# Bucketed attention and two gated layers on one core: P x V in bursts of two groups, the bucket projection in float32 column tiles, other ranks

## The chip, the cores and the metric

One core of a Trainium2 chip runs the whole program. The metric is the device time of one execution in microseconds. Three executions of the kernel before took 786.24, 788.03 and 2870.33 us; the median is 788.03 us. A fourth execution, the profiled one, took 786.92 us.

## The reference

Two batches of eight heads, 768 positions, head size 64. Each query and key gets a 6-bit bucket from the signs of its projection; only pairs of one bucket attend. Two dense layers follow over 1536 tokens, 512 wide inside and out, 2048 in the middle.

```python
q_bits = (einsum('bhsd,dk->bhsk', q, proj) > 0); k_bits likewise
mask   = q_bucket[:, :, :, None] == k_bucket[:, :, None, :]
scores = where(mask, scale * q @ k.T, -1e9)
attn   = softmax(scores); x = attn @ v                       # float32
h = x @ w_in;  P = a0 + a1 h + a2 h^2 + a3 h^3;  Q = 1 + |b0||h| + |b1|h^2
x = (P / (Q + 1e-6)) @ w_out
h = x @ w_in2; out = (h * clip(h + 3, 0, 6) / 6) @ w_out2
```

All inputs and the output are float32.

## The kernel before

**Attention** is cut into 48 groups, `group(g)`: head g // 3, 256 query rows, handled as two tiles of 128 rows (rr = 0, 1). Per group: S, four matmuls per row tile (`s_mm`, L326 and L329); M, the row maximum on DVE (L333); E, the exponential on ACT (L55, p<-s); NV and A, small sums; N, the normalisation of a 128x768 tile on POOL (L354), twice; P, twelve transposes on TensorE (`p_mm`, L362, tiles tt); H, three copies of the transposed tiles out of PSUM on ACT or DVE (`p_copy`, L55 and L372, tiles pt); V, twelve float32 matmuls (`v_mm`, L380), which put the two row tiles in two column halves of the array, 64 columns each; OC and VA, copies of the result on ACT and DVE; for odd heads XH and XL, the split into a high and a low part on POOL (L403, L409).

**Heads** come in pairs, `pair(pr)`. Per head: LQ, loads of q and k; TP, six transposes (`tp_mm`, L215); TH, the rounded high part by ACT (two halves of 384); TL, the low part by DVE (two halves, L58, tl<-tp,qsc,th). Per pair: Z, the projection onto the six directions, in the high and low parts: twelve 384-column matmuls over the whole array (`z_mm`, L254); ZB, the comparison to bits on DVE (L259, two halves). SPH, SPL and SB are DMAs on SP's queue that copy high parts, low parts and bits into the operands q1, q2, k1, k2 of the scores; all of them stand in SP's queue in one order.

**Layers.** There are 96 steps of 24 matmuls of 512 columns (L432 in, L500 out). Weights are converted from raw float32 to two rounded parts, in 64 units: two passes on ACT (L110, L114), a shift on DVE (L119), an addition on POOL (L123), the high part on ACT or POOL (L131, L133), the low part on DVE or POOL (L138). The first NPRE units have room during attention, the next NMID when its early buffers are released.

**What sets the order.** All work is put in a table with a rank (group number times `W_SLOT` plus an offset `OFF`), engines with costs `W`, and dependencies. `ordered()` places the lowest rank that is ready on a free engine of its model and writes each engine's instructions in that order. On the chip each engine goes through its own list in order and waits for what the next instruction needs. Buffers are rings: four PSUM banks "T" are shared by tp, z, tt and o; two double banks "S" hold scores; six pt tiles hold transposed probabilities. `start()` writes head 0 by hand; `fill` puts in a few matmuls on zeros.

Of the kernel before, what the change touches and what calls it, by code (L numbers as in the profile page):

```python
# [14 lines left out]
NB = 6  # L15
# [10 lines left out]
NPRE = 11  # L26
NMID = 8
WARM = 8
CVS = (1, 2, 5, 11, 17, 23, 29, 35, 39, 42, 43)
RING = {"raw": 3, "cvd": 3, "t1": 2, "t2": 3, "t3": 2, "t4": 1, "gh": 2, "gl": 2}  # L30

W = {"S": 0.70, "M": 0.87, "E": 0.89, "NV": 0.53, "A": 0.28, "N": 0.97, "P": 0.44, "H": 0.59, "H_D": 0.66, "V": 1.4, "OC": 0.30,
# [8 lines left out]
W_SLOT = 4.7626  # L41

OFF = {"S": -2.838, "rr": 3.521, "M": -6.776, "E": -11.597, "NV": -11.654, "A": -3.446, "N": -8.05, "P": 10.877, "H": -13.583, "V": 14.339,
       "OC": -19.289, "VA": -4.457, "XH": 12.347, "XL": -6.444, "TP": 13.65, "Z": 6.62, "c": 2.102, "SPH": -7.318, "SPL": -23.623, "SB": -8.428,
       "LQ": -20.758, "LV": 0.663, "ld": -12.347, "cf": 7.841}
AHEAD = 3.8243
FILL = {("TP", 1, 1): 3, ("S", 1, 1): 6}
RINGS = {"T": 4, "S": 2, "p": 6, "pt": 6}


def body(tc, q, k, v, proj, moe_w_in, moe_w_out, moe_a, moe_b, moe2_w_in, moe2_w_out, out):
    nc = tc.nc

    def act(out, in_, func=ACTF.Copy, **kw):
        nc.scalar.activation(out=out, in_=in_, func=func, **kw)  # L55
# [85 lines left out]
    nat, spl, hl, lr, live = {}, {}, {}, {}, {}  # L141
# [54 lines left out]
    for _ in range(WARM):  # L196
        nc.tensor.matmul(out=warm, lhsT=zfill[:, 0:128], rhs=zfill[:, 128:512], start=True, stop=True)

# [9 lines left out]
    thr = cpool.tile([128, 2], F32, name="thr")  # L208

# [8 lines left out]
    def tp_hi(hd, n):  # L218
        if n == 0:
            hl[hd] = tuple(ate.tile([128, S], F32R, name=f"t{x}", tag=f"t{x}{hd % 2}") for x in "hl")  # L220
        act(hl[hd][0][:, n * 384:(n + 1) * 384], live[("tp", hd, n)], scale=qsc)

    def tp_full(hd, n):
        full = live[("tf", hd, n)] = ate.tile([128, 384], F32, name="tf", tag="tf", bufs=2)
        act(full, live.pop(("tp", hd, n)), scale=qsc)

    def tp_lo(hd, n):
        th, tl = (t[:, n * 384:(n + 1) * 384] for t in hl[hd])
        if ("tf", hd, n) in live:
            nc.gpsimd.tensor_tensor(out=tl, in0=live.pop(("tf", hd, n)), in1=f(th), op=ALU.subtract)  # L230
        else:
            stt(tl, live.pop(("tp", hd, n)), qsc, f(th), ALU.mult, ALU.subtract)
# [14 lines left out]
    def z_mm(pr, n, heads=(0, 1)):  # L247
        z = live[("z", pr, n)] = psum.tile([128, 384], F32, name="z", tag="T", bufs=4)
        ops = []
# [6 lines left out]
    def z_bits(pr, n):  # L256
        if n == 0:
            live["bt"] = ate.tile([128, S], F32R, name="bt")
        nc.vector.tensor_scalar(out=live["bt"][:, n * 384:(n + 1) * 384], in0=live.pop(("z", pr, n)), scalar1=thr[:, 0:1],  # L259
                                scalar2=thr[:, 1:2], op0=ALU.is_gt, op1=ALU.mult)  # L260

    def spread_bits(hd):
        for i in range(2):
            o = 64 * (hd % 2) + 32 * i
            nc.sync.dma_start(out=f(lr[hd][2 * i + 1])[64:KP], in_=f(live["bt"])[o:o + 2 * NB])
# [7 lines left out]
    def start():  # L273
# [21 lines left out]
        for n in range(2):  # L295
            z_mm(0, n, (0,))
            z_bits(0, n)
# [537 lines left out]
```

## Time and profile before

| | us |
|---|---|
| median of three executions | 788.03 |
| profiled execution, device time | 786.92 |
| its span, first to last instruction | 785.1 |
| TensorE matmul busy | 771.5 (98%) |
| TensorE weight load busy | 654.2 (83%) |
| DVE busy | 553.9 (71%) |
| ACT busy | 482.0 (61%) |
| POOL busy | 352.5 (45%) |

The span falls into attention (to about 260 us), and the layers after it, which begin to mix in from 246 us. A busy share over the whole span mixes the two, so the rows further down are cut by stretch. Matmul ends are modelled; where a price is wanted, the difference between starts in the timeline is the safer reading.

### The profile page before, as it was taken

How to read it: one execution, taken by the hardware profiler on the slowest of the kernel's cores; microseconds unless marked ns; L12 is line 12 of the kernel's file. 1: busy time of each engine (PE TensorE's matmuls, PEld its weight loads, DVE VectorE, ACT ScalarE, POOL GpSimd, SP SyncE). 2: the span in 40 equal slices, each digit the busy share in tenths (PEclk: the TensorE clock that was granted, in tenths of full speed). 3: DMA queues.
4: the chain of work that ended last, by engine and by line, in shares of the span. 5: the costliest groups of instructions: out<-in, count | busy, mean ns of one | idle time of the engine just before them, and what ended most of it. 6: DMA issues, size and time to landing. Idle time of an engine off the chain costs nothing.

```text
span 785.1 us, 12730 instructions
## 1 busy us (share of the span) xinstructions
PE 771.5 (98%) x4629; PEld 654.2 (83%) x4629; DVE 553.9 (71%) x927; ACT 482.0 (61%) x893; POOL 352.5 (45%) x413
## 2 busy tenths in 40 slices
PE   8999999999999999999999999999999999999997
PEld 7888989999998887788888888888888888888886
DVE  7898988887788999999989999987622322232222
ACT  6887976677767888966557789887522322222221
POOL 3798985665677746722224476876500000000000
PEclk9999999999999999999999999999999999999999
DMA  7986786465330324400002033336100100010001
GB/s 190 228 223 166 195 217 152 116 144 121 75 86 21 114 82 131 125 14 1 0 1 78 4 108 108 108 108 198 69 1 1 54 1 1 1 53 1 1 0 55
DMA packets 46767, 65.78 MB, mean 84 GB/s; under 512 B 28808, under 2 KB 30856, under 8 KB 46704
## 3 DMA queue, kind: packets, MB, share of 16 engines
q1 hardware_dynamic: 45920, 64.76, 29.8%
q8 instruction: 37, 0.61, 0.3%
q10 hardware_dynamic: 784, 0.20, 0.1%
q14 instruction: 26, 0.21, 0.1%
HBM read 43.00 MB, written 3.15 MB: 59 GB/s over the span
## 4 chain that ended last, share of the span: by engine, by line
PE 85%; DVE 8%; ACT 4%; DMA 2%; issue 1%; POOL 1%; SPq 0%; ACTq 0%; POOLq 0%
PE h L432 30%; PE acc L500 30%; PE tt L362 8%; PE o L380 8%; PE s L326 4%; PE s L329 3%; DVE t L58 3%; PE z L254 2%; PE tp L215 1%; DVE stat L333 1%; DVE cvd L119 1%; ACT t L55 1%; DVE wo_0l L138 1%; DMA q<-th 1%; DVE r L58 1%
## 5 line engine op out<-in xcount | busy, mean ns | idle before, releaser
L354 POOL TENSOR_SCALAR p<-p,stat 128x768 f32<-128x768 f32 x96 | 95.7, 1004 | 35.4 <-DVE stat L350 21.7
L58 DVE SCALAR_TENSOR_TENSOR t<-t,h 128x512 f32<-128x512 f32 x48 | 33.1, 689 | 107.7 <-ACT t L55 107.7
L55 ACT ACTIVATE t<-h,cbias 128x512 f32<-128x512 f32 x48 | 33.1, 689 | 122.7 <-PE h L432 122.7
L123 POOL TENSOR_TENSOR cvd<-cvd,raw 128x512 int32<-128x512 int32 x64 | 89.2, 1396 | 42.1 <-DVE cvd L119 20.1
L489 POOL TENSOR_TENSOR gl<-t,gh 128x512 fp32r<-128x512 f32 x48 | 63.3, 1318 | 98.2 <-ACT gh L55 90.8
L55 ACT ACTIVATE p<-s,stat 128x768 f32<-128x768 f32 x96 | 85.9, 899 | 11.7 <-DVE stat L333 10.3
L333 DVE TENSOR_REDUCE stat<-s 128x1 f32<-128x768 f32 x96 | 89.4, 953 | 3.8 <-PE s L329 2.4
L55 ACT ACTIVATE gh<-t 128x512 fp32r<-128x512 f32 x96 | 60.5, 630 | 47.7 <-PE acc L500 41.6
L362 PE MATMUL tt<-ident,p 128*128 128x128 f32 x576 | 84.7, 277 | 1.4 <-DVE bt L259 0.9
L362 PEld LDWEIGHTS tt<-ident,p 128*128 128x128 f32 x576 | 66.7, 140 | 11.8 <-issue 5.1
L380 PE MATMUL o<-pt,nv 128*64 128x128 f32 x1152 | 73.5, 277 | 0.3 <-DVE bt L259 0.3
L489 DVE TENSOR_TENSOR gl<-t,gh 128x512 fp32r<-128x512 f32 x48 | 37.5, 781 | 51.3 <-PE acc L500 47.8
L58 DVE SCALAR_TENSOR_TENSOR t<-t,coef,h 128x512 f32<-128x512 f32 x96 | 71.4, 744 | 1.7
L380 PEld LDWEIGHTS o<-pt,nv 128*64 128x64 f32 x1152 | 61.9, 137 | 10.0 <-issue 6.1
L58 DVE SCALAR_TENSOR_TENSOR t<-t,r 128x512 f32<-128x512 f32 x96 | 65.8, 685 | 4.7 <-ACT r L55 2.3
L372 DVE COPY pt<-tt 128x512 f32<-128x512 f32 x75 | 50.7, 686 | 25.0 <-PE tt L362 24.7
L55 ACT ACTIVATE pt<-tt 128x512 f32<-128x512 f32 x69 | 40.8, 595 | 39.5 <-PE tt L362 39.0
L326 PE MATMUL s<-k,q 128*128 128x384 f32 x192 | 56.1, 373 | 1.7 <-ACT p L55 1.7
L500 PE MATMUL acc<-gh,wo_0h 128*128 128x512 f32 x192 | 54.6, 391 | 2.2 <-ACT gh L55 2.2
L500 PE MATMUL acc<-gl,wo_0h 128*128 128x512 f32 x192 | 54.4, 390 | 0.0
L500 PE MATMUL acc<-gh,wo_0l 128*128 128x512 f32 x192 | 54.3, 389 | 0.0
L500 PE MATMUL acc<-wo_0h,gh 128*128 128x512 f32 x192 | 54.2, 389 | 0.0
(124 smaller groups left out, 1850.9 us busy)
## 6 DMA issues: line engine op xcount, KB each, us to landing
raw<-in_moe_w_in_dram SPq DMA_DIRECT2D x32, 512.0 KB
raw<-in_moe_w_out_dram SPq DMA_DIRECT2D x32, 512.0 KB
q<-th SPq DMA_DIRECT2D x30, 192.0 KB
k<-th SPq DMA_DIRECT2D x30, 192.0 KB
nqk<-in_q_dram SPq DMA_DIRECT2D x16, 192.0 KB
nv<-in_v_dram SPq DMA_DIRECT2D x16, 192.0 KB
out_dram<-o SPq DMA_DIRECT2D x12, 256.0 KB
nqk<-in_k_dram SPq DMA_DIRECT2D x15, 192.0 KB
```

The source lines that it names most:

```text
L55: nc.scalar.activation(out=out, in_=in_, func=func, **kw)
L58: nc.vector.scalar_tensor_tensor(out=out, in0=in0, scalar=scalar, in1=in1, op0=op0, op1=op1)
L123: nc.gpsimd.tensor_tensor(out=d.bitcast(I32), in0=d.bitcast(I32), in1=raw[:, :, 0], op=ALU.add)
L326: nc.tensor.matmul(out=ps[:, n, 0:384], lhsT=q1[:, rs], rhs=k1[:, n * 384:(n + 1) * 384], start=True, stop=False)
L333: nc.vector.tensor_reduce(out=stats[g % 4][:, rr, 0:1], in_=sps[(g, rr)][:, :, 0:384], axis=AX.XY, op=ALU.max, negate=True)
L354: nc.gpsimd.tensor_scalar(out=pt, in0=pt, scalar1=st[:, rr, 4:5], scalar2=st[:, rr, 5:6], op0=ALU.mult, op1=ALU.add)
L362: nc.tensor.transpose(ps[:, kt, rr], ptile[(g, rr)][:, c:c + 128], ident)
L372: nc.vector.tensor_copy(out=pt, in_=live.pop(("p", g, i)))
L380: nc.tensor.matmul(out=o[64 * rr:64 * rr + 64], lhsT=vs[:, kt], rhs=pt[:, kt % 2, rr * 128:rr * 128 + 128], start=(kt == 0), stop=(kt == R ...
L432: nc.tensor.matmul(out=ps, lhsT=w[:, ws], rhs=x[:, cols(m)], start=(n == 0), stop=(n == 3 * KD - 1))
L489: (nc.gpsimd if eng == "POOL" else nc.vector).tensor_tensor(out=e["gl"], in0=e["2"], in1=f(e["gh"]), op=ALU.subtract)
L500: nc.tensor.matmul(out=acc["o"][i], lhsT=lhsT, rhs=rhs, start=(t == 0 and n == 0), stop=(t == NF - 1 and n == 2))
```

## The change

- **V in bursts.** One V entry now does two groups, 24 matmuls in a row, and comes with the odd group. It takes two T banks at once and waits for six pt tiles; the pt ring grows from 6 to 9. The load of v waits for the burst that uses the older v.
- **Z in float32 column tiles.** `z_mm` is one entry per pair: four float32 matmuls of 384 columns with 32 output columns each, one for each (head, half), at the four column positions of the array. ZB is one comparison per pair over all four. The weights `zw` and thresholds `thr2` are made at the end of `start()`: a memset and two multiplications on DVE, thirteen memsets on POOL, two tiny matmuls.
- **The split.** TF (ACT) first copies the scaled transposes to SBUF in float32, two halves; TH then is one 768-wide rounding on ACT or POOL, TL one 768-wide subtraction on DVE or POOL. Z needs TF only. Head 0 keeps the old form.
- **SB** is four DMAs per head (12x384) where it was two (12x768).
- **Conversion.** 13 units ahead (NPRE), then 6 (NMID); before 11 and 8. In the built program 16 of the first passes on ACT stand among the exponentials of the first 36 groups, before 14 among those of the first 18 groups; at the last attention copy 19 units have passed ACT and POOL's addition, before 17.
- **Warming.** Sixteen float32 matmuls on zeros of 32 rows and 64 columns of the array, 192 moving columns each, and a DVE transpose of zeros come before the first loads land.
- **Ranks.** `W`, `OFF`, `W_SLOT` and `AHEAD` have other values, so each engine's list is in another order.

In the built program ACT does 81 and DVE 63 of the 144 H copies (69 and 75 before); of the 15 later heads, TH stands 14 times on ACT and once on POOL, TL 8 times on DVE and 7 times on POOL.

```diff
-NPRE = 11
-NMID = 8
+NPRE = 13
+NMID = 6
-RINGS = {"T": 4, "S": 2, "p": 6, "pt": 6}
+RINGS = {"T": 4, "S": 2, "p": 6, "pt": 9}
...
+    warm = [psum.tile([128, 192], F32, name="warm", tag="T", bufs=4) for _ in range(4)]
+    for _ in range(2):
+        for i in range(4):
+            rows = slice(32 * i, 32 * i + 32)
+            for c in (0, 64):
+                nc.tensor.matmul(out=warm[i][c:c + 64], lhsT=f(zfill)[rows, 0:64], rhs=f(zfill)[rows, 64:256], start=True, stop=True)
...
+    def tp_full(hd, n):
+        if n == 0:
+            tf[hd] = ate.tile([128, S], F32, name="tf", tag=f"tf{hd % 2}")
+        act(tf[hd][:, n * 384:(n + 1) * 384], live.pop(("tp", hd, n)), scale=qsc)
...
+    def z_mm(pr, heads=(0, 1)):
+        z = live[("z", pr)] = psum.tile([128, 384], F32, name="z", tag="T", bufs=4)
         for par in heads:
-            th, tl = hl[2 * pr + par]
-            ops += [(zl[0][par], th), (zl[1][par], th), (zl[0][par], tl)]
-        for i, (w, t) in enumerate(ops):
-            nc.tensor.matmul(out=z, lhsT=w, rhs=t[:, n * 384:(n + 1) * 384], start=(i == 0), stop=(i == len(ops) - 1))
+            for n in range(2):
+                c = 32 * (2 * par + n)
+                nc.tensor.matmul(out=z[c:c + 32], lhsT=zw, rhs=tf[2 * pr + par][:, n * 384:(n + 1) * 384], start=True, stop=True,
+                                 tile_position=(0, c))
...
+            r = (g0 - 5) * T + OFF["Z"]
+            add(("Z", pr), ("PE", W["Z"]), r, [("TF", hd, n) for hd in heads for n in range(2)] + [("SB", 2 * pr - 1)],
+                lambda e: z_mm(pr, which), takes=("T",))
...
+            if g % 2:
+                two = (g - 1, g)
+                add(("V", g), ("PE", W["V"]), b + OFF["V"], [("H", x, i) for x in two for i in range(3)] + [("LV", hd), ("LV", (g - 1) // 3)],
+                    lambda e: [v_mm(x) for x in two], takes=("T", "T"), frees=tuple(("H", x, i) for x in two for i in range(3)))
```

TensorE's list, some way into attention, before (s scores, tt transposes of probabilities, o P x V, z projection, tp transposes of q and k):

```order
L362 MATMUL tt<-ident,p 128x128 x8
L380 MATMUL o<-pt,nv 64x128 x12
L326 MATMUL s<-k_600,q_598 128x384 x2
L329 MATMUL s<-k_601,q_599 128x384 x2
L326 MATMUL s<-k_600,q_598 128x384 x2
L329 MATMUL s<-k_601,q_599 128x384 x2
L254 MATMUL z<-th,zl 128x384 x2
L254 MATMUL z<-tl,zl 128x384
L254 MATMUL z<-th,zl 128x384 x2
L254 MATMUL z<-tl,zl 128x384
L362 MATMUL tt<-ident,p 128x128 x12
```

The same stretch of TensorE's list in the change:

```order
L415 MATMUL o<-pt,nv 64x128 x24
L397 MATMUL tt<-ident,p 128x128 x8
L361 MATMUL s<-k_1530,q_1528 128x384 x2
L364 MATMUL s<-k_1531,q_1529 128x384 x2
L361 MATMUL s<-k_1530,q_1528 128x384 x2
L364 MATMUL s<-k_1531,q_1529 128x384 x2
L397 MATMUL tt<-ident,p 128x128 x4
L263 MATMUL z<-tf,zw 32x384 x4
L226 MATMUL tp<-ident,nqk 128x128 x6
L397 MATMUL tt<-ident,p 128x128 x8
```

A burst holds 24 matmuls where it held 12, and four z matmuls of 32 columns stand where a half of the old projection (six of 128) stood; the other half is gone.

POOL's list at the start of the program, from the last copy that makes head 0's operands on, before (k is an operand of the scores, stat small statistics, p the probabilities of the first groups):

```order
L285 TENSOR_SCALAR k_164<-tl 64x384
L345 TENSOR_SCALAR stat_149<-stat_149 128x2 x2
L354 TENSOR_SCALAR p<-p,stat_149 128x768 x2
L345 TENSOR_SCALAR stat_150<-stat_150 128x2 x2
L123 TENSOR_TENSOR cvd<-cvd,raw 128x512
L354 TENSOR_SCALAR p<-p,stat_150 128x768 x2
```

POOL's list in the change, from the end of the thirteen memsets that follow that copy on:

```order
L288 MEMSET trow_172 1x12
L243 TENSOR_TENSOR tl<-tf,th 128x768
L380 TENSOR_SCALAR stat_174<-stat_174 128x2 x2
L237 TENSOR_SCALAR th<-tf 128x768
L243 TENSOR_TENSOR tl<-tf,th 128x768
L380 TENSOR_SCALAR stat_175<-stat_175 128x2 x2
L389 TENSOR_SCALAR p<-p,stat_174 128x768 x2
L389 TENSOR_SCALAR p<-p,stat_175 128x768
```

The low parts of heads 1 and 2 and one high part now stand ahead of the first normalisation, and the first conversion has moved behind it.

## Rows read from the trace of the kernel before

**Rows 1.** The page, part 1: busy us, share of the span, instructions

```profile
span 785.1 us, 12730 instructions
PE 771.5 (98%) x4629; PEld 654.2 (83%) x4629; DVE 553.9 (71%) x927; ACT 482.0 (61%) x893; POOL 352.5 (45%) x413
```

**Rows 2.** Windows: stretch, length, busy PE, PEld, DVE, ACT, POOL, clock, DMA share, GB/s

```profile
12.00:120.00 108.00, 103.46 (x953) 92.78 (x953) 96.55 (x182) 88.66 (x187) 89.75 (x125) 1.00 0.82 208
120.00:240.00 120.00, 120.00 (x1192) 109.42 (x1188) 96.96 (x183) 80.14 (x177) 72.70 (x123) 1.00 0.46 109
240.00:340.00 100.00, 97.19 (x517) 78.23 (x514) 93.00 (x146) 85.81 (x154) 67.18 (x60) 1.00 0.30 95
340.00:785.10 445.10, 440.73 (x1945) 364.61 (x1943) 261.02 (x384) 221.18 (x368) 118.69 (x95) 1.00 0.13 42
```

**Rows 3.** What matmuls waited for, 12 to 120 us: total, times, longest

```profile
PE s L326 <- ACT p L55: 1.7, 3, 1.1
PE z L254 <- DVE tl L58: 1.2, 2, 0.8
PE tt L362 <- DVE bt L259: 0.9, 1, 0.9
PE tt L362 <- POOL p L354: 0.5, 1, 0.5
```

**Rows 4.** The same, 240 to 345 us

```profile
PE acc L500 <- ACT gh L55: 2.2, 3, 1.2
PE h L432 <- DVE t L58: 0.6, 2, 0.3
```

**Rows 5.** Timeline of TensorE in attention: start us, busy us, work

```profile
146.16 0.51 PE L329 MATMUL s<-k,q 76*128 76x384 f32 x2
146.51 0.60 PE L362 MATMUL tt<-ident,p 128*128 128x128 f32 x4
146.95 0.49 PE L215 MATMUL tp<-ident,nqk 128*128 128x128 f32 x3
...
147.64 0.51 PE L329 MATMUL s<-k,q 76*128 76x384 f32 x2
148.07 1.53 PE L380 MATMUL o<-pt,nv 128*64 128x128 f32 x24
149.53 1.09 PE L362 MATMUL tt<-ident,p 128*128 128x128 f32 x8
...
150.82 0.34 PE L254 MATMUL z<-tl,zl 128*128 128x384 f32 x1
...
151.54 0.33 PE L326 MATMUL s<-k,q 128*128 128x384 f32 x1
```

**Rows 6.** Groups by line: busy us, mean ns of one, idle before

```profile
L489 POOL TENSOR_TENSOR gl<-t,gh 128x512 fp32r<-128x512 f32 x48 | 63.3, 1318 | 98.2 <-ACT gh L55 90.8 <-issue 7.4
L354 POOL TENSOR_SCALAR p<-p,stat 128x768 f32<-128x768 f32 x96 | 95.7, 1004 | 35.4 <-DVE stat L350 21.7 <-PE s L326 7.2 <-PE s L329 4.4
L55 ACT ACTIVATE q<-th 64x768 fp32r<-64x768 f32 x2 | 1.6, 835 | 0.0
L55 ACT ACTIVATE pt<-tt 128x512 f32<-128x512 f32 x69 | 40.8, 595 | 39.5 <-PE tt L362 39.0
L119 DVE TENSOR_SCALAR cvd<-cvd 128x512 int32<-128x512 int32 x64 | 34.3, 547 | 0.9 <-ACT cvd L55 0.9
```

**Rows 7.** Windows: a full stretch of attention, the weak stretch of the layers

```profile
80.00:100.00 20.00, 20.00 (x197) 18.40 (x196) 19.14 (x36) 18.03 (x40) 19.18 (x26) 1.00 0.74 201
300.00:320.00 20.00, 18.17 (x78) 14.04 (x77) 19.82 (x29) 16.98 (x31) 14.38 (x11) 1.00 0.48 155
```

**Rows 8.** Timeline of TensorE and of POOL at the start

```profile
1.45 2.93 PE L197 MATMUL warm<-zfill 128*128 128x384 f32 x8 [1.45 <-DVE zfill L159]
4.78 1.51 PE L215 MATMUL tp<-ident,nqk 128*128 128x128 f32 x6 [0.40 <-DMA nqk<-in_q_dram]
...
15.94 1.95 POOL L354 TENSOR_SCALAR p<-p,stat 128x768 f32<-128x768 f32 x2 [1.03 <-DVE stat L350]
```

More of the change, by code (lines that the diff above doesn't have):

```diff
@@ L208, in body @@
     thr = cpool.tile([128, 2], F32, name="thr")
+    zw = ate.tile([128, 32], F32, name="zw")
+    trow2 = ate.tile([1, 2, 128], F32, name="trow2")
+    thr2 = cpool.tile([128, 2], F32, name="thr2")
     def tp_mm(hd, n):
@@ L262, in spread_bits, with z_bits @@
+    def z_bits(pr, heads=(0, 1)):
+        live["bt"] = ate.tile([128, 384], F32R, name="bt", tag="bt")
+        rows = slice(64 * heads[0], 64 * heads[-1] + 64)
+        nc.vector.tensor_scalar(out=live["bt"][rows], in0=live.pop(("z", pr))[rows], scalar1=thr2[rows, 0:1],
+                                scalar2=thr2[rows, 1:2], op0=ALU.is_gt, op1=ALU.mult)
     def spread_bits(hd):
         for i in range(2):
-            o = 64 * (hd % 2) + 32 * i
-            nc.sync.dma_start(out=f(lr[hd][2 * i + 1])[64:KP], in_=f(live["bt"])[o:o + 2 * NB])
+            for n in range(2):
+                o = 64 * (hd % 2) + 32 * n + 2 * NB * i
+                nc.sync.dma_start(out=f(lr[hd][2 * i + 1])[64:KP, n * 384:(n + 1) * 384], in_=f(live["bt"])[o:o + 2 * NB])
@@ new lines, in z_setup @@
+    def z_setup():
+        nc.vector.memset(zw, 0.0)
+        for isk in range(2):
+            rows = slice(64 * isk, 64 * isk + 64)
+            nc.vector.tensor_tensor(out=zw[rows, 2 * NB * isk:2 * NB * isk + 2 * NB].rearrange("p (a b) -> p a b", a=2),
+                                    in0=pj[rows].unsqueeze(1).to_broadcast([64, 2, NB]), in1=sgn[rows], op=ALU.mult)
+        nc.gpsimd.memset(trow2, 0.0)
+        for j in range(4):
+            nc.gpsimd.memset(trow2[:, 0, 32 * j + NB:32 * j + 3 * NB], -TINY)
+            nc.gpsimd.memset(trow2[:, 1, 32 * j:32 * j + 2 * NB], 1.0)
+            nc.gpsimd.memset(trow2[:, 1, 32 * j + 2 * NB:32 * j + 4 * NB], -BIG)
@@ L267, in fill, with z_thr @@
+    def z_thr():
+        pst = psum.tile([128, 2], F32, name="pst", tag="T", bufs=4)
+        for i in range(2):
+            nc.tensor.matmul(out=pst[:, i:i + 1], lhsT=trow2[:, i, :], rhs=one1, start=True, stop=True)
+        nc.vector.tensor_copy(out=thr2, in_=pst)
     def fill(n):
@@ L294, in start @@
         nc.vector.tensor_copy(out=thr, in_=pst)
+        bt = ate.tile([128, S], F32R, name="bt0")
         for n in range(2):
-            z_mm(0, n, (0,))
-            z_bits(0, n)
+            c = slice(n * 384, (n + 1) * 384)
+            z = psum.tile([128, 384], F32, name="z", tag="T", bufs=4)
+            for i, (w, t) in enumerate(((0, th), (1, th), (0, tl))):
+                nc.tensor.matmul(out=z, lhsT=zl[w][0], rhs=t[:, c], start=(i == 0), stop=(i == 2))
+            nc.vector.tensor_scalar(out=bt[:, c], in0=z, scalar1=thr[:, 0:1], scalar2=thr[:, 1:2], op0=ALU.is_gt, op1=ALU.mult)
         act(q1[64:128], tl[0:64])
-        nc.vector.tensor_copy(out=k2[64:KP], in_=f(live["bt"])[32:32 + 2 * NB])
-        nc.vector.tensor_copy(out=q2[64:KP], in_=f(live["bt"])[0:2 * NB])
+        nc.vector.tensor_copy(out=k2[64:KP], in_=f(bt)[32:32 + 2 * NB])
+        nc.vector.tensor_copy(out=q2[64:KP], in_=f(bt)[0:2 * NB])
+        z_setup()
+        z_thr()
     def coef_load():
```

84 lines of the change are left out of this document (37 added, 47 removed), and 2 rows, old and new, of the table W.

## The prediction

> **What bounds the kernel now.** I read the page first: TensorE is busy for 98% of the span, no other engine for more than 71% [rows 1]. A busy TensorE need not be at its limit, so the stretches come next [rows 2]. From 120 to 240 us matmuls are busy for all of 120 us and weight loads for 91% of it, with DVE at 81%, ACT at 67% and POOL at 61%; no matmul waits for another engine there that the waits would list. That stretch is TensorE's own work. From 12 to 120 us 4.5 us of matmul time are missing and weight loads fall to 86%; the waits name four causes, together 4.3 us: scores for ACT's exponentials, z for DVE's low part, transposes for DVE's bits, transposes for POOL [rows 3]. From 240 to 340 us another 2.8 us are missing, all waits for the element-wise chain of the first layer [rows 4], in a stretch where DVE is busy for 19.8 of 20 us [rows 7]. After 340 us TensorE is full to the end. The end is therefore set by TensorE's list: what leaves that list shortens the run one for one, until another engine takes its place; some 7 us of waits can come or go besides.
>
> **P x V in bursts of two.** In the timeline [rows 5] the 24 records of a burst start at 148.07 and the next work at 149.53: 1.46 us. What would they take without a change of tile shape? Two of the records run beside each other (two column halves), so there are twelve pairs of 128 moving columns. Four transposes, with 128 moving columns each, take 0.44 us (146.51 to 146.95), 0.11 us each, so twelve pairs take 1.31. So 0.15 is spent behind the burst. Ahead of it, two score matmuls take 0.43 (147.64 to 148.07) where the same two take 0.35 ahead of transposes (146.16 to 146.51): 0.08. Behind it, eight transposes and the first two z matmuls take 1.29 (149.53 to 150.82) where eight at 0.11 and two at 0.18 make 1.23: 0.06. A burst costs about 0.30 us beyond its work. With 24 bursts in place of 48, 24 x 0.30 = 7.2 us go. Bounds: 0.15 (the gap behind alone) gives 3.6, and nothing at all if two groups' matmuls in a row also pay 0.30 between them; inside a burst no such gap shows, so I take 7.2.
>
> The Trainium skill's page "TensorEngine Tiling (Array Packing)", section "Tiling Modes", says that changing the mode, not the tile, drains the engine. The 0.30 us around each burst agree; by the page the second group of a burst pays nothing, which is the 7.2.
>
> What a burst could cost elsewhere: it waits for the last of six copies (H), and all of TensorE's list stands behind it. But the last copy is used only in the second half, about 1.3 us into the burst, so the copy has more time than before. It holds two of four T banks until two copies each by ACT and DVE; I put that at nothing while scores, which use other banks, follow.
>
> **Z in float32.** Four z matmuls take 0.72 us (150.82 to 151.54), 0.18 each [rows 5]. Of 96, 90 go: 16.2 us. What comes is eight bursts. A float32 matmul is two records (24 for twelve, rows 5); one with 384 columns takes 2 x 3 x 0.11 = 0.65 at that pace. If the four column tiles run beside each other a burst takes 0.65 + 0.30 = 0.95, eight 7.6, and 8.6 us go. Two at a time give 1.61, eight 12.9, and 3.3 go; one after another 2.92, eight 23.4, and 7.2 us come. The trace shows two column tiles beside each other and nothing on four; the row is nearest to "as many as there are", so I take 8.6.
>
> The page "TensorE: Matmul & The Clock Gate", Part 3, speaks against the full gain: it measured 2.38 times, not three times, for three column tiles. By that share a z burst would take 1.12 us as an estimate, and 7.2 us would go instead of 8.6; no run here shows it.
>
> **Start.** POOL's first normalisation starts at 15.94 us [rows 8]. Now thirteen memsets, two low parts (1.98 each, 1.5 times the 512-wide 1.318), one high part (1.00) and two rows of statistics stand ahead of it [rows 6], and ACT's 0.84 for the high part ahead of those. From about 13.7, when ACT can have that high part, POOL is through with these at about 20: 4 us late. The first conversion, which stood behind the first normalisation, has moved back, so much of this is caught up within a few groups. The sixteen matmuls on zeros start when the eight old ones end (1.45 + 2.93); tp starts at 4.78 now. At the pace of that stretch (eight matmuls of 384 columns in 2.93 us, so some 0.35 each where later 0.18) one of 192 columns and two records takes about 0.65: 1.3 together if eight run beside each other, so tp is about 1 us late; if only column pairs do, 5.2 and 4.8 late. I take 1.5 us for the whole start, between -2 (it is all caught up, and TensorE reaches its later pace earlier) and +5.
>
> **Waits.** Z needs only ACT's float32 copy, no longer DVE's low part, and there is one comparison where there were two: the rows on tl and bt, 2.1 us [rows 3], should go; I take -2. Two more units are converted before the layers start; each takes a shift of 0.55 us from DVE [rows 6] and at least as much for the low part out of the stretch in which DVE is full. I take -2 of the 2.8 us [rows 4], between 0 and -2.8. Against that, ACT gets 14 x 0.84 + 12 x 0.60 + four conversion passes at about 0.60, some 21 us; on 168.8 of 228 us from 12 to 240 [rows 2] this is 190 of about 214, 89%. POOL gets 7 x 1.98 + 1.00 + two additions of about 1.32, 17.5 us: 180 of 214, 84%. DVE gets less of everything. From 80 to 100 us DVE, ACT and POOL were 96, 90 and 96% busy and matmuls lost nothing [rows 7], so such loads can be carried; still, less slack will cost a little. I take +1 for 12 to 240 us, between 0 and +10. The two extra DMAs per head for the bits cost SP's queue time only; SP's next transfers stand behind them, and z now comes earlier in a head's chain, so I take nothing.
>
> **Sum**, against the span of 785.1: -7.2 - 8.6 + 1.5 - 2 - 2 + 1 = -17.3, so 767.8. The median of the runs shown is 788.03, 2.9 above the span (the profiled execution itself took 786.92, 1.8 above). On that footing: **770.7 us**. Changes within 2% (772.3 to 803.8) are about what a measurement of this kernel can't tell from none, so the forecast stands near that edge.
>
> **Rivals.**
> - *Waits go altogether.* The new ranks and the lighter DVE take all 7.1 us of rows 3 and 4 and the start is caught up: -7.2 - 8.6 - 7.1 = -22.9, 765.1. For it: three of the four causes of rows 3 are touched. Against: ACT is fuller.
> - *The four column tiles don't run beside each other.* Two at a time: +5.3, 776.0; one at a time: +15.8, 786.5. For it: only pairs are in the trace.
> - *ACT takes TensorE's place.* If its 190 us can be packed only to 85% (it reached 82% from 12 to 120 us, where scores waited for it), the stretch takes 224 us and not 214: 780.7. Against: the 90% of rows 7.
> - *The matmuls on zeros run in pairs or singly* and everything starts late: +4 to +9, 775 to 780.
> - *POOL holds up the path: slower.* Each low part of 1.98 us stands in POOL's list ahead of normalisations, and transposes wait for those. If all 17.5 us that POOL gains and the 4 us at the start fall on TensorE's list, the 15.8 saved are overtaken: +21.5 - 15.8 = +5.7, 793.7. It decides when about three quarters of POOL's new time lands on the path; to pass 2% more would have to be lost than POOL gains. Against: POOL has 39% free from 120 to 240 us.
>
> **How the numbers follow.** Forecast (766 to 775) 0.56; waits gone 0.14; z tiles not side by side 0.09; ACT 0.13; zeros 0.04; POOL, slower 0.04. Likeliest: 770.7. The range of 763 to 781 holds the forecast, most of the first rival, the ACT case, the paired z and the late start. Faster than 772.3: some seven tenths of the forecast and all of the first rival, 0.55. Slower by over 2%: 0.03, the tail of the POOL case. Within: 0.42.
>
> **What would show each step.** Right: bursts of 48 records with about 2.9 us between starts; z of eight records (four matmuls) with about 0.95; six groups in about 2.1 us less of TensorE's time between 120 and 240 us (3 x 0.30 and 12 x 0.18 - 0.95), still without waits; fewer waits between 300 and 330 us. Wrong: z at 1.6 or more; a gap in the middle of a burst; scores that wait for ACT p or transposes that wait for POOL p through all of attention; tp later than 6 us. If TensorE has new waits of over 10 us before the layers, the step "one for one" is what failed.

## The result, and the profile of the changed kernel

The changed kernel takes 780.08 us (median of 4 runs, 778.77 to 780.26) against 787.45 us for the kernel before on the same chip: ratio 0.9908, 95% interval 0.9888 to 0.9927. The ratio leaves out one execution of the kernel before, which took 2870.33 us. The change is 7.4 us faster where 17.3 us were forecast; 780.1 lies inside the range of 763 to 781, close to its upper end, and the gain is below the 2% line.

The page of the change, its first part (busy us, share of the span, instructions), beside [rows 1]:

```profile
span 778.4 us, 12794 instructions
PE 764.8 (98%) x4635; PEld 642.0 (82%) x4635; DVE 534.4 (69%) x894; ACT 489.2 (63%) x908; POOL 380.2 (49%) x441
```

The windows of the change by stretch (length; busy time and records of PE, PEld, DVE, ACT, POOL; granted clock, DMA share, GB/s), beside [rows 2]:

```profile
12.00:120.00 108.00, 105.18 (x990) 93.18 (x992) 87.31 (x160) 91.43 (x193) 89.86 (x124) 0.97 0.71 183
120.00:240.00 120.00, 118.23 (x1219) 106.66 (x1216) 96.98 (x184) 98.97 (x214) 100.90 (x143) 1.00 0.54 141
240.00:340.00 100.00, 100.00 (x485) 82.04 (x484) 92.76 (x146) 80.40 (x142) 67.43 (x58) 1.00 0.27 85
340.00:778.40 438.40, 434.19 (x1891) 354.46 (x1890) 250.28 (x367) 213.47 (x354) 116.39 (x93) 1.00 0.13 43
```

TensorE is still busy for 98%. Three things differ from before: the clock is 0.97 in the first stretch, 1.77 us of matmul time are missing from 120 to 240 us where none was, and none is missing from 240 to 340 us where 2.8 us were. ACT and POOL have risen from 80 and 73 us to 99 and 101 us of the 120 us in the second stretch.

What TensorE waited for in the change (total us, times, longest): 4 to 12 us (one row), 12 to 120 us (two rows), 120 to 240 us (two rows); from 240 to 345 us there is no row.

```profile
PE pst L293 <- POOL trow L286: 3.3, 1, 3.3
...
PE s L361 <- ACT p L55: 2.6, 6, 1.0
PE tt L397 <- POOL stat L380: 0.3, 1, 0.3
...
PE s L361 <- ACT p L55: 1.5, 4, 0.9
PE tt L397 <- ACT tf L55: 0.3, 1, 0.3
```

Beside [rows 3] the waits for DVE's low part and bits are gone, and the scores wait longer for the exponentials (4.1 us where 1.7 stood). Beside [rows 4] the waits of the layers are gone. The 3.3 us of L293 are new.

The timeline of TensorE in attention (start us, busy us, work): a burst of z and one of P x V, each with what follows.

```profile
27.75 0.52 PE L364 MATMUL s<-k,q 76*128 76x384 f32 x2
28.20 0.85 PE L263 MATMUL z<-tf,zw 128*32 128x384 f32 x8
28.98 0.62 PE L361 MATMUL s<-k,q 128*128 128x384 f32 x2
...
33.25 0.52 PE L364 MATMUL s<-k,q 76*128 76x384 f32 x2
33.70 2.84 PE L415 MATMUL o<-pt,nv 128*64 128x128 f32 x48
36.48 0.62 PE L361 MATMUL s<-k,q 128*128 128x384 f32 x2
```

The z burst takes 0.78 us from its start to the next work's; the two scores ahead of it take 0.45 where 0.35 is their own time, so 0.88 with its entry (0.95 was forecast). The P x V burst takes 2.78, 2.88 with its entry (2.92 was forecast), and its 48 records are one row without a gap.

So the two bursts are about as forecast, and yet the gain is 10 us smaller than forecast. To find the place, the start of each layer step (every twelfth matmul of L467, of L432 before) was set against the trace before. The change leads by 8.6 us at step 4, by 12.1 at step 24, and by only 6.9 at step 95, the last: 5.2 us are lost again in a stretch in which nothing of the change runs and no matmul waits. The other loss is at the very start: its first score begins at 14.82 us, 3.7 us later than in the trace before:

```profile
11.16 0.52 PE L326 MATMUL s<-k,q 128*128 128x384 f32 x2
```

### The profile page after: what moved, and what is told of

Its sections match the earlier page's. It is cut to its first block, busy times and chain, and to the rows that moved or that the text cites. A ratio compares the mean times of both kernels' runs of the same rounds, so it can differ in the third digit from the quotient of the medians.

```text
span 778.4 us, 12794 instructions
## 1 busy us (share of the span) xinstructions
PE 764.8 (98%) x4635; PEld 642.0 (82%) x4635; DVE 534.4 (69%) x894; ACT 489.2 (63%) x908; POOL 380.2 (49%) x441
## 4 chain that ended last, share of the span: by engine, by line
PE 87%; ACT 6%; DVE 4%; POOL 1%; issue 1%; DMA 1%; ACTq 0%; POOLq 0%; DVEq 0%
PE acc L535 34%; PE h L467 34%; PE o L415 6%; PE tt L397 5%; PE s L361 3%; PE s L364 3%; ACT p L55 3%; DVE stat L368 2%; PE tp L226 1%; DMA raw<-in_moe_w_in_dram 1%; DVE pt L407 1%; ACT pt L55 1%; ACT raw L55 1%; ACT cvd L55 0%; PE z L263 0%
## 5 line engine op out<-in xcount | busy, mean ns | idle before, releaser
L389 POOL TENSOR_SCALAR p<-p,stat 128x768 f32<-128x768 f32 x96 | 101.8, 1067 | 9.8 <-DVE stat L385 4.9
L397 PE MATMUL tt<-ident,p 128*128 128x128 f32 x576 | 75.1, 274 | 0.5 <-ACT tf L55 0.3
L415 PE MATMUL o<-pt,nv 128*64 128x128 f32 x1152 | 68.2, 275 | 0.0
L361 PE MATMUL s<-k,q 128*128 128x384 f32 x192 | 57.8, 382 | 4.1 <-ACT p L55 4.1
L55 ACT ACTIVATE pt<-tt 128x512 f32<-128x512 f32 x81 | 47.2, 601 | 18.2 <-PE tt L397 18.0
L535 PE MATMUL acc<-wo_0h,gl 128*128 128x512 f32 x192 | 54.9, 392 | 0.0
L535 PE MATMUL acc<-wo_0l,gh 128*128 128x512 f32 x192 | 54.8, 392 | 0.0
```

Source lines behind the costliest of these rows:

```text
L361: nc.tensor.matmul(out=ps[:, n, 0:384], lhsT=q1[:, rs], rhs=k1[:, n * 384:(n + 1) * 384], start=True, stop=False)
L389: nc.gpsimd.tensor_scalar(out=pt, in0=pt, scalar1=st[:, rr, 4:5], scalar2=st[:, rr, 5:6], op0=ALU.mult, op1=ALU.add)
L397: nc.tensor.transpose(ps[:, kt, rr], ptile[(g, rr)][:, c:c + 128], ident)
L415: nc.tensor.matmul(out=o[64 * rr:64 * rr + 64], lhsT=vs[:, kt], rhs=pt[:, kt % 2, rr * 128:rr * 128 + 128], start=(kt == 0), stop=(kt == R ...
L535: nc.tensor.matmul(out=acc["o"][i], lhsT=lhsT, rhs=rhs, start=(t == 0 and n == 0), stop=(t == NF - 1 and n == 2))
```

## The experiments

All ratios are to the kernel before, timed beside it on the same chip. Where an edit changes the table of work, the lists of all engines are sorted anew. "The repaired change" below is the change with both side effects undone, the kernel of the second study.

### Study 1: the layers' pace and the start

**What is slower in the layers.** The table of matmuls of the change from 345 us on, shapes and operands apart (records | busy us, mean ns of one | idle before), four of its rows:

```profile
L535 PE MATMUL acc<-wo_0h,gh 128*128 128x512 f32 x192 | 54.9, 393 | 0.0
...
L467 PE MATMUL h<-xh,wi_3h 128*128 128x512 f32 x80 | 31.6, 394 | 0.0
...
L467 PE MATMUL h<-xh,wi_2h 128*128 128x512 f32 x80 | 31.2, 391 | 0.0
L467 PE MATMUL h<-xh,wi_1h 128*128 128x512 f32 x80 | 31.1, 389 | 0.0
```

In the kernel before all such rows have 389 ns:

```profile
L432 PE MATMUL h<-xh,wi_3h 128*128 128x512 f32 x80 | 31.1, 389 | 0.0
```

Matmuls with weights of the units wi1 keep that, those of wi3 take 5 ns more; neighbours overlap, and from start to start the two are 227 and 233 ns apart. The slow ones are those whose weights lie in the last weight pool, `wpool2`: all units of wi3, one in four of wi2, half of wo. The change brings one new tile into the constants, `thr2`, 8 bytes per partition in a 32-byte slot. Behind it all pools that fill the memory from the left (x, the steps' intermediates, the first two weight pools) moved up by 32 bytes, counted past a multiple of 2048. `wpool2` is laid from the right end and did not move. Before, x starts at byte 2080 and `wpool2` at 174112 of each partition, both 32 past a multiple of 2048; in the change x starts at 2112, 64 past one. Four kernels move the two against each other, by a slot more or by the pad behind `wpool2`'s last tile:

```diff
# a_gap: the change;  b_gap: the kernel before, behind thr
+    cpool.tile([128, 2], F32, name="gap")
# a_w2: the change (wpool2 moves down by 32 bytes)
-    wpool[wplace[u]].tile([128, 512 + (496 if u == order[-1] and hl == "l" else 0)], ...
+    wpool[wplace[u]].tile([128, 512 + (504 if u == order[-1] and hl == "l" else 0)], ...
# a_same: the change (wpool2 moves up by 32 bytes)
-    wpool[wplace[u]].tile([128, 512 + (496 if u == order[-1] and hl == "l" else 0)], ...
+    wpool[wplace[u]].tile([128, 512 + (488 if u == order[-1] and hl == "l" else 0)], ...
```

One slot more behind `thr2`: x moves to 96, the difference to `wpool2` is 64 bytes.

> The changed kernel with one unused 8-byte tile (a slot of 32 bytes) behind thr2, so that x, the first weights and the element-wise tiles stand 32 bytes further on, as they stood relative to the last weights before the change; nothing else differs. Theory (placement): the layers' matmuls of the weights in the last pool run at 233 ns instead of 227 because these weights and x now differ by 32 bytes in their place modulo 64; the gap brings 227 back everywhere, from step 24 to the end nothing is lost, and the time falls by 4.7 to 5.3 us, to about 775. Rival (something else is slower: the clock's grant of 0.996, the larger pool of first weights): the pace stays at 229 to 230 on the mean and the time at 780.

Measured: 777.83 us, 0.9884 [0.9863, 0.9905], 2 us less than the change, though the two intervals overlap. The lead over the kernel before is the safer sign: it falls by 3.3 us from step 24 to step 95, where the change's falls by 5.2. Four rows of its matmul table from 345 us on:

```profile
L536 PE MATMUL acc<-wo_0h,gh 128*128 128x512 f32 x192 | 54.8, 392 | 0.0
...
L468 PE MATMUL h<-xl,wi_3h 128*128 128x512 f32 x80 | 31.6, 395 | 0.0
L468 PE MATMUL h<-xh,wi_3l 128*128 128x512 f32 x80 | 31.3, 391 | 0.0
...
L468 PE MATMUL h<-xh,wi_2l 128*128 128x512 f32 x80 | 31.1, 389 | 0.0
```

The pattern changes (wi2's low part is back at 389, wi3's at 391), but not all comes back.

`wpool2` 32 bytes lower, which is again a difference of 64, by the other side:

> The changed kernel with the last pool of weights moved by 32 bytes instead (8 more pad elements in its last tile), so that now weights, x and element-wise tiles all stand at multiples of 64. If what counts is that the two operands of a matmul have the same place modulo 64, all matmuls run at 227 ns and the time falls by 5 us to 775, as with the gap. If multiples of 64 are slow in themselves, or the last pool is slow for another reason, the pace stays at 229 to 233 and the time at 780.

Measured: 777.98 us, 0.9888 [0.9868, 0.9907]: the same as a_gap, and its lead falls by 3.3 us too. In these two pairs it is the difference of the two places that counts, not the place of either.

`wpool2` 32 bytes higher, a difference of 0 as before:

> The changed kernel with 8 pad elements fewer in the last tile of the last pool, so that its weights stand at 64 bytes modulo 2048, as x, the first weights and the element-wise tiles do in the change (before, all stood at 32 modulo 2048; in the change the last pool stayed at 32). Theory (same place modulo 2048): all layer matmuls run at 227 ns and the time falls by 5 us, to about 775, and falls further than with a_gap and a_w2, whose difference was 64 bytes and which got back 2.3 us only. Rival (the size of the last pool or what lies in it): the pace of its weights stays between 229 and 233 and the time at 777 to 780.

Measured: 773.63 us, 0.9829 [0.9812, 0.9845], 6.2 us less than the change by the two ratios. Its lead over the kernel before stands at 13.3 us from step 16 to step 95: nothing is lost in the layers any more, and the row of wi3 is back at 389:

```profile
L467 PE MATMUL h<-xh,wi_3h 128*128 128x512 f32 x80 | 31.1, 389 | 0.0
```

The kernel before with the slot, and nothing else, a difference of 32 bytes:

> The kernel before with an unused tile of one 32-byte slot in the constants' pool: x, the first weights and the element-wise tiles move by 32 bytes, the last pool of weights doesn't. No instruction differs. Theory (same place): the layer matmuls that read the last pool's weights slow down from 227 to 233 ns from about 395 us on, and the run gets 5 us longer, about 792. Rival: nothing, 787.

Measured: 792.2 us, 1.0065 [1.0047, 1.0083]: 5.1 us slower. From step 24 to step 95 it loses 5.3 us to the kernel without the slot, and its rows are those of the change.

```profile
L501 PE MATMUL acc<-wo_0h,gh 128*128 128x512 f32 x192 | 54.9, 393 | 0.0
...
L433 PE MATMUL h<-xh,wi_3h 128*128 128x512 f32 x80 | 31.6, 394 | 0.0
```

So the slot alone costs 5 to 6 us, in either kernel. Only differences of 0, 32 and 64 bytes were tried; on which grid the place counts, and what in the chip makes it count, stays open.

**The start.** TensorE at the start of the change, and POOL there (of its twelve small memsets the first and the last):

```profile
4.30 1.07 PE L203 MATMUL warm<-zfill 32*64 32x192 f32 x32
5.42 0.84 PE L226 MATMUL tp<-ident,nqk 128*128 128x128 f32 x6
...
11.58 1.01 PE L293 MATMUL pst<-one,trow 1*128 1x1 f32 x4 [3.34 <-POOL trow L286]
12.52 1.54 PE L226 MATMUL tp<-ident,nqk 128*128 128x128 f32 x6
...
14.82 0.84 PE L361 MATMUL s<-k,q 128*128 128x384 f32 x2
```

```profile
10.35 0.62 POOL L284 MEMSET trow<- 1x256 f32 x1
11.04 0.10 POOL L286 MEMSET trow<- 1x12 f32 x1
...
11.51 0.10 POOL L288 MEMSET trow<- 1x12 f32 x1
```

The sixteen matmuls on zeros take 1.07 us, which fits eight beside each other (1.3 in the prediction) and not pairs (5.2), and tp begins 0.64 us later than in [rows 8]. Then `z_thr`, two tiny matmuls which turn `trow2` into the new thresholds, stands in TensorE's list ahead of head 1's transposes. Its rows are written by the thirteen memsets at the end of POOL's work on head 0 (L284 to L288). TensorE stands idle for 3.34 us until they are done, and then works at half pace. Windows of the change (columns as above):

```profile
4.00:11.40 7.40, 4.18 (x50) 2.83 (x48) 5.13 (x15) 3.68 (x6) 4.25 (x16) 1.00 0.71 185
11.40:18.20 6.80, 6.62 (x23) 4.93 (x24) 1.51 (x3) 2.87 (x5) 2.01 (x6) 0.50 0.52 147
```

Behind the idle time the granted clock is 0.50, the lower of its two levels, for 6.8 us; the six transposes of 12.52 take 1.54 us where those of 5.42 take 0.84.

The 3.7 us by which the first score is late hold some chance. b_gap has the instructions of the kernel before, and yet its six transposes are fast from the beginning, and its first score begins at 8.98 us where the trace before has 11.16:

```profile
4.74 0.85 PE L216 MATMUL tp<-ident,nqk 128*128 128x128 f32 x6 [0.37 <-DMA nqk<-in_q_dram]
```

The wait doesn't hang on that: a_same, whose matmuls on zeros take 1.67 us, has it as well (3.33 us). One kernel moves the memsets ahead of head 0's work, beside those of the old rows:

```diff
     trow2 = ate.tile([1, 2, 128], F32, name="trow2")
+    nc.gpsimd.memset(trow2, 0.0)
+    for j in range(4): ...                # the twelve memsets of L286 to L288
...
     def z_setup():
...
-        nc.gpsimd.memset(trow2, 0.0)
-        for j in range(4): ...
```

> The changed kernel with POOL's thirteen memsets of trow2 issued near the program's beginning instead of behind head 0's copies. Theory (start): TensorE's 3.3 us of waiting for trow2 at 8.2 us go, the clock does not fall to half between 11.5 and 18.3 us, the first scores start at about 11 us and not at 14.8, and the whole run is 4 to 5 us shorter, about 775.5. Rival (paid back anyway): the lag of the start is used up by waits for POOL and ACT that exist in the first ten groups in any case (against before, the lag falls from 4.7 us at group 6 to 0.2 at group 10); then the first scores come earlier but the end moves by less than 1.5 us.

Measured: 776.77 us, 0.987 [0.985, 0.989], 3.0 us less than the change by the ratios. TensorE there, with L293 no longer waiting and the granted clock at 1.000 over the run (how much of the gain is the wait and how much the clock was not separated):

```profile
8.44 0.60 PE L293 MATMUL pst<-one,trow 1*128 1x1 f32 x4
8.97 0.87 PE L231 MATMUL tp<-ident,nqk 128*128 128x128 f32 x6
...
10.21 0.51 PE L361 MATMUL s<-k,q 128*128 128x384 f32 x2
```

The early memsets together with the slot of a_gap:

> Both edits together: the gap of 32 bytes and the early memsets. If both theories hold the gains add up: 780.1 - 5.0 - 4.5, about 770.5, which is the forecast of the prediction. If only one holds, 775; if neither, 780.

Measured: 773.14 us, 0.9828 [0.9813, 0.9842]. From the change that is 6.3 us, somewhat more than a_gap and a_early alone (1.9 and 3.0) add up to; the intervals of the three allow for it.

### Study 2: the repaired change, and its parts undone

a_same and a_early together:

> The changed kernel with both mends: memsets of trow2 early, and the last pool at the same place modulo 2048. If both theories hold: 776.8 (early memsets alone) less 5, about 771.5, 2% under the kernel before, which is where the prediction had put the change. If the gain of one uses up the other's: 774 or more.

Measured: 770.57 us, 0.9787 [0.9773, 0.9802]; 9.5 us less than the change, as a_same and a_early alone add up to (6.2 and 3.0). That is the time that was forecast for the change itself. Its lead over the kernel before is 11.9 us at step 4 and 16.5 from step 16 to step 95, and its granted clock is 1.000 in all four executions.

**P x V one group at a time** again, with the old wait of v's load and a cost of 1.42 in place of 2.85 in the table; the rest is as in the repaired change:

```diff
-            if g % 2:
-                add(("V", g), ..., lambda e: [v_mm(x) for x in two], takes=("T", "T"), ...)
+            add(("V", g), ..., lambda e: v_mm(g), takes=("T",), ...)
```

> f_base with P x V one group at a time again (rank, wait for v and ring of T as before; nine pt tiles stay). The step of the prediction: 24 more bursts at 0.30 us each are 7.2 us more than f_base. Rival (the bursts' gain is lost to waits, because a burst holds two T banks and six pt tiles): 3 us or less more than f_base.

Measured: 777.59 us, 0.988 [0.9855, 0.9905]: 7.0 us more than the repaired change. Its timeline has the old bursts back:

```profile
108.23 1.53 PE L415 MATMUL o<-pt,nv 128*64 128x128 f32 x24
109.69 0.62 PE L361 MATMUL s<-k,q 128*128 128x384 f32 x2
```

1.46 us from start to start, as in [rows 5]. Two of them take 0.14 us more than one burst of 2.78, and the entry of 0.10 is paid once more: 24 times 0.24 make 5.8 us by the rows. The two profiled executions differ by 5.8 as well, the medians by 7.0 with about 2.3 either way.

**The old projection of the bits**, two halves per pair of heads, with what goes with it: a comparison for each half, two transfers of bits per head, and the wait for the low part:

```diff
-    def z_mm(pr, heads=(0, 1)):           # four float32 matmuls of 32 columns
+    def z_mm(pr, n, heads=(0, 1)):        # six matmuls of 128 columns on the two parts
...
-    ztr = ate.tile([128, 512], F32, name="ztr")
-    nc.vector.transpose(out=ztr, in_=f(zfill))
```

> The repaired change (both side effects undone) with the projection of the bits done the old way: two halves of six 128-column matmuls each, two comparisons, one transfer of bits per row block; the V bursts stay in pairs, and the vector engine's transposition of zeros at the start is left out for room. Theory 1 (the term Z of the sum is right and nothing hides it): the old halves come back at about 1.09 us and the new burst of about 0.8 to 0.95 goes, so 8.6 to 9.5 us more than the repaired change's 770.6: 779 to 780. Theory 2 (the waits on the low part come back as well): 2 more, 781 to 783. Theory 3 (attention is held by the exponentials on the scalar engine, so that a shorter z only lets TensorE wait longer): less than 5 more, 771 to 775.

Measured: 777.22 us, 0.9869 [0.985, 0.9888]: 6.4 us more than the repaired change by the two ratios, with about 2 either way: below the first theory, and at its lower end within the third. A half of z in its timeline:

```profile
145.68 0.59 PE L268 MATMUL z<-th,zl 128*128 128x384 f32 x2
146.11 0.34 PE L268 MATMUL z<-tl,zl 128*128 128x384 f32 x1
146.28 0.51 PE L268 MATMUL z<-th,zl 128*128 128x384 f32 x2
146.63 0.34 PE L268 MATMUL z<-tl,zl 128*128 128x384 f32 x1
```

A half takes 1.1 us of TensorE, a pair of heads 2.2 where the new burst takes 0.88: seven pairs make 9.2. Some 6 of these arrived at the end. The profiled executions can't say where the rest went: their spans differ by 8.0, and 2.6 of those were already there at the first transposes of probabilities (24.80 us against 22.21), behind a wait of 1.36 us and a window of clock 0.66. The granted clock is 0.995 to 0.997 in all four executions and 1.000 in all four of the repaired change, so a part of the 6.4 us is the clock's and not the projection's own. The term is of the forecast's sign and at most about three quarters of its size.

**11 units converted ahead** in place of 13, 8 in the layers:

```diff
-NPRE = 13
-NMID = 6
+NPRE = 11
+NMID = 8
```

> The repaired change with 11 units converted in attention and 8 in the layers, as before. Theory 1 (the two units take the vector engine out of its full stretch between 300 and 330 us): TensorE's waits there come back, 2 to 3.6 us more than 770.6: 772.5 to 774.2, with rows on the element-wise chain between 240 and 345 us. Theory 2 (the layers' waits went for another reason, the new ranks among them): 770 to 771 and no such rows. Theory 3 (the two conversions cost attention what they save behind it): 770 to 771, with the rows back and fewer waits for the exponentials in attention.

Measured: 769.23 us, 0.9774 [0.9749, 0.9799], not to be told from the repaired change. The layers' waits did not come back; the window of this kernel from 240 to 345 us:

```profile
240.00:345.00 105.00, 105.00 (x501) 86.80 (x500) 99.03 (x155) 88.67 (x155) 72.72 (x61) 1.00 0.30 90
```

DVE is busy for 99.03 of 105 us in it and yet no matmul time is missing. The 288 matmuls of steps 4 to 16 take 65.3 us from the first start to the last, as in the repaired change; in the kernel before they take 69.9. The first theory falls: the two units are worth nothing that shows.

**Without the sixteen matmuls on zeros:**

```diff
-    warm = [psum.tile([128, 192], F32, name="warm", tag="T", bufs=4) for _ in range(4)]
-    for _ in range(2): ...                # sixteen matmuls, 32 rows by 64 columns
-    ztr = ate.tile([128, 512], F32, name="ztr")
-    nc.vector.transpose(out=ztr, in_=f(zfill))
```

> The repaired change without the sixteen small matmuls on zeros and without the transposition of zeros on the vector engine (the eight old matmuls on zeros stay). Theory 1 (the forms only stand ahead of the first transposes): tp begins 0.6 us sooner, at about 4.8, 769.5 to 770.6. Theory 2 (they hold TensorE's granted clock at full through the start): the clock is at half for a while between 5 and 16 us and the scores begin later, 1 to 4 us more: 771.5 to 774.5.

Measured: 769.55 us, 0.9774 [0.975, 0.9798]: no difference. Its TensorE at the start:

```profile
4.82 1.51 PE L221 MATMUL tp<-ident,nqk 128*128 128x128 f32 x6 [0.45 <-DMA nqk<-in_q_dram]
...
12.66 0.84 PE L351 MATMUL s<-k,q 128*128 128x384 f32 x2
```

tp begins at 4.82 and not at 5.96 as in the repaired change, but at the slow pace (1.51 us for six), and the scores begin 1.8 us later (12.66 against 10.82). At the first transposes of probabilities 0.7 us of that is left (22.91 against 22.21), at the first layer step none (235.68 against 235.92). The slow pace doesn't follow from leaving the zeros out: f_best, the last kernel below, has none either, and its tp is fast:

```profile
4.78 0.87 PE L221 MATMUL tp<-ident,nqk 128*128 128x128 f32 x6 [0.41 <-DMA nqk<-in_q_dram]
```

So the first theory has the start of tp right, the second is not shown, and neither piece reaches the end.

**The old ranks**, that is slot, table and lead of the kernel before, with the new operations:

```diff
-W_SLOT = 4.9815
-OFF = {"S": -3.045, "rr": 1.278, "M": -4.361, ...}
-AHEAD = 0.8458
+W_SLOT = 4.7626
+OFF = {"S": -2.838, "rr": 3.521, "M": -6.776, ...}
+AHEAD = 3.8243
```

> The repaired change with the slot, the ranks and the lead of the kernel before (the table that sorts the work of attention), everything else as in the repaired change. Theory 1 (TensorE's list is what counts, and the order of the rest is worth a few waits): within 1.5 us of 770.6. Theory 2 (the new ranks are what lets the scalar engine carry its added work, a part of the change that the sum held at nothing): rows of scores waiting for exponentials through attention, 3 to 15 us more, 774 to 786.

Measured: 781.96 us, 0.9939 [0.9919, 0.9959], 11.4 us more than the repaired change. The profiled execution is the longest of its five (786.19 us). In it the scores of attention wait 9.0 us for the exponentials (6.4 and 2.6), and from 240 to 345 us 2.1 us of waits are back, with NPRE at 13. Is it the lead of the conversions or the ranks of attention? First the old lead alone:

```diff
-AHEAD = 0.8458
+AHEAD = 3.8243
```

> The repaired change with one number of the table put back: the lead with which the layers' conversions are sorted ahead of their use, 3.82 pairs of steps in place of 0.85. The kernel with 11 units converted ahead had no wait of TensorE between 240 and 345 us, so the two units are not what took the 2.8 us of before away there. Theory 1 (the shorter lead did: shifts and low parts of conversions now stand behind the chain of the running step): waits on the element-wise chain come back between 240 and 345 us, 1.3 to 3.6 us more than 770.6: 771.9 to 774.2. Theory 2 (neither the lead nor the units, but the order of attention's tail): within 1 us of 770.6, no such rows.

Measured: 769.31 us, 0.9773 [0.9756, 0.9789]: no difference, and no row of waits from 240 to 345 us. The lead is not it. Then the old slot and ranks with the new lead:

```diff
-W_SLOT = 4.9815
-OFF = {"S": -3.045, "rr": 1.278, "M": -4.361, ...}
+W_SLOT = 4.7626
+OFF = {"S": -2.838, "rr": 3.521, "M": -6.776, ...}
```

> The repaired change with the old slot and the old ranks of attention's operations, but with the new lead of the conversions. The kernel with all the old numbers lost 11.4 us to the repaired change, of which its lead can hold only what the layers lose (2.1 us of waits between 240 and 345 us). Theory 1 (the ranks of attention hold the most): 778 to 781, scores waiting for exponentials as long as there (6.4 and 2.6 us), no waits in the layers. Theory 2 (the lead holds it): within 2 us of 770.6.

Measured: 788.03 us, 1.0015 [1.0003, 1.0027], 18 us more than the repaired change: the whole gain. What TensorE waits for in this kernel, the longest row of 8 to 120 us, the longest of 120 to 240 us, and all of 240 to 345 us:

```profile
PE s L361 <- ACT p L55: 6.4, 7, 1.7
...
PE s L361 <- ACT p L55: 2.8, 4, 1.8
...
PE acc L535 <- ACT gh L55: 1.6, 1, 1.6
PE h L467 <- DVE t L58: 1.4, 1, 1.4
PE acc L535 <- POOL gl L524: 1.0, 1, 1.0
```

Under the old ranks of attention the layers' waits are there at either lead, under the new ones they are absent at either lead (f_ahead) and with 11 or 13 units (f_pre11). From start to start the 288 matmuls of steps 4 to 16 say the same: 68.0 us in f_ranks and 70.6 in f_off, 65.3 in f_pre11 and 65.7 in f_ahead. The ranks of attention's own work take the waits away. Which of the ranks does it was not tried. Under the old ranks the new lead is 6 us slower than the old one; about 2.6 of these are in the layers, the rest is open. In both traces the granted clock is also at 0.50 twice in attention (from 47 us on in both, and from 118 us in f_ranks and 132 in f_off), so a part of what the ranks cost is the clock's. The expectation of f_off had the place of the loss right and missed at least 7 us of its size, the 4.0 us of the layers among them.

**The best version**: the repaired change with 11 units and without the matmuls on zeros.

> The repaired change with both parts left out that measured as nothing: 11 units converted ahead and 8 in the layers, and no small matmuls on zeros. Theory 1 (the two are independent and worth at most 1 us each): 768 to 770.5. Theory 2 (they differ from the repaired change by chance alone): 770 to 771.

Measured: 768.69 us, 0.9769 [0.975, 0.9788], the lowest of all, though its interval overlaps that of the repaired change. It beats both the kernel before and the change.

## Why the prediction was wrong, step by step

- **"What leaves TensorE's list shortens the run one for one."** It holds for P x V and roughly for z: with the side effects undone the kernel takes 770.57 us, and 770.7 was forecast. The number was one for a kernel that only has the change's work in it, and that it fits so closely is in part luck. By the traces of the two kernels, the repaired change leads by 11.9 us at step 4, where the sum has 15.3 for the start and attention, and gains another 4.6 in the first layer steps, where it has 2.
- **P x V, -7.2.** Right: 7.0 us by the medians of f_v1, 5.8 by its rows. The Trainium skill's page "TensorEngine Tiling (Array Packing)", section "Tiling Modes", by which changing the mode, and not just the tile, drains the engine, agrees with the trace: the second group of a burst pays nothing (one row of 48 records, 2.78 us).
- **Z, -8.6.** The mechanism is right: four column tiles run beside each other. The burst is a little cheaper than forecast (0.88 against 0.95), and what reached the end, 6.4 us, is less than the term. The estimate of 1.12 us for a burst, drawn from the Trainium skill's page "TensorE: Matmul & The Clock Gate", Part 3, was too high, but not by the page's share: 2.38 for three tiles would be 3.2 for four, and the burst of 0.78 is 3.3 times the pace of one after another (an estimate of 0.65 each by the rows, 2.6 for four). The 0.30 us on top of it were too much; 0.10 of them shows ahead of the burst.
- **Start, +1.5.** Mis-sized, and by the wrong mechanism. The prediction counted the memsets as thirteen instructions on POOL ahead of the first normalisation, and looked for their price there; the first normalisation, forecast for about 20 us, starts at 24.13 in the change and at 19.19 in the repaired change, so that reading of POOL's list was sound. It did not ask what stands behind them on TensorE: `z_thr` waits for them in a list that runs in order, with head 1's transposes behind it. The wait of 3.34 us and the half clock behind it put the first score 3.7 us late; a_early gives 3.0 us back. The forecast's own worry, the matmuls on zeros, was right in kind (eight beside each other, tp 0.64 us later) and worth nothing at the end (f_nowarm).
- **Waits on low parts and bits, -2.** Right: the rows of [rows 3] are gone.
- **Layers' waits, -2.** Too small, and not by the step given. The rows of 2.8 us went altogether, and from start to start the matmuls of steps 4 to 16 take 4.6 us less than before (65.3 against 69.9). Each of the five waits is about 0.27 us longer between starts than in its row: 0.16 because a matmul's record (389 ns) reaches past the next start (227 ns), and 0.11 in the start behind it. The two units do nothing there (f_pre11), nor does the lead (f_ahead); the ranks of attention do (f_off).
- **New waits, +1.** Too low: scores wait 4.1 us for the exponentials in the change where 1.7 us stood, and 1.77 us of matmul time are missing from 120 to 240 us where none was. ACT's load from 12 to 240 us came out as forecast (190 us), POOL's higher (191 against 180). The rival "ACT takes TensorE's place" is in the trace as these 4.1 us, "POOL holds up the path" as 0.3 us in attention and the 3.3 at the start; neither decides.
- **New ranks, nothing.** The sum gave them no term. They are worth 11 to 18 us with this work (f_ranks, f_off), a part of it through the clock: the old ranks eat two thirds or all of the gain. That the forecast for the rest came out at 770.6 rests on a table that fits; the prediction assumed this and did not say so.
- **What had no step at all: +5 to +6.** One new tile of 8 bytes shifted x against the last weight pool by 32 bytes. The prediction costed operations, queues and waits, and took the stretch after 340 us as full to the end without asking at which pace. a_same gives 6.2 us back, b_gap costs the old kernel 5.1. This is the largest part of the 10 us that are missing, and the start is most of the rest (6.2 and 3.0 make 9.2).

The chances stood at 0.42 for "within 2%", so the result was not ruled out; but the cases from which they came (z in pairs, ACT full, POOL late) are not what made it.

## What to carry to other kernels

When a change adds even a tiny constant, compare where the large operands lie before and after: an allocation that grows from both ends can shift the two operands of every matmul against each other, and it shows as a few nanoseconds in the mean of rows that the change doesn't touch. For every small new instruction on one engine, look for the first consumer of its result and for what is queued behind that consumer; an idle TensorE can also cost the granted clock behind it (here 6.8 us at half the clock behind 3.3 us of waiting). Where the price of a wait is wanted, compare starts over the same matmuls and not only rows of waits. A table of ranks belongs to the operations for which it was made, so a sum that changes the operations has to say that the table fits them.

## What the runs showed of the hardware that was not expected

- The same float32r matmul of 512 columns comes every 227 ns or every 233 ns, by where its weights lie relative to its moving operand: at a difference of 0 bytes (counted past a multiple of 2048) all take the 227, at 32 bytes the worst take 233, and at 64 bytes the pattern is milder (2 us of about 6 back). In rows: 389, 391 and 394 ns mean.
- Sixteen float32 matmuls of 32 rows by 64 columns went through eight tiles of the array beside each other: 32 records of 192 columns in 1.07 us in the change, and in 1.67 us in f_base, where the transposes behind them are still slow in part (1.18 us for six).
- When TensorE reaches its fast pace at the start differs from execution to execution, and the profile's clock doesn't show it. The first record of the clock in a trace lies at 4.6 us in the change, 6.7 in f_base, 13.9 in f_nowarm, 10.8 in the kernel before and 4.4 in b_gap, which has the same instructions. Six transposes ahead of that record take about 1.5 us, behind it about 0.85, and a window ahead of it reads 1.00 because it holds no record. In the thirteen traces with the matmuls on zeros the first record lies between 4.6 and 7.6 us, in the four without them at 4.4, 4.8, 10.8 and 13.9: they may keep late ones away, but four traces don't show it.
